# A decode layer's last weight row: two half-row loads, two half-width sums, one store

## The chip, the cores and the metric

The kernel runs on one core of a Trainium2 chip. The metric is the device time of one execution in microseconds (us), lower is better. Times below are medians over runs; a profiled execution is one run with the hardware profiler on. In the profile PE is the matrix engine, PEld its weight loads, DVE the vector engine, ACT the scalar engine, POOL the general-purpose engine and SP the engine that issues most of the transfers.

## The reference

One decode step of a parallel layer: one token `x` of 1024 values, an attention branch with a window of the last 4096 cached positions, and an MLP branch, summed with `x`. Everything is bf16.

```python
x = A_x                                   # [1, 1, 1024]
xn = _layernorm(x)
# attention: 32 heads of 128, 4 key/value heads, window W = 4096 of 65536
q = (xn @ wq)                             # wq [1024, 4096]
p = softmax(q . k[-W:] * 128 ** -0.5)
attn = (p . v[-W:]).reshape(4096) @ wo    # wo [4096, 1024]
# MLP
y = _layernorm(xn)
h = gelu(y @ w1 + b1)                     # w1 [1024, 3584]
mlp = h @ w2 + b2                         # w2 [3584, 1024]
out = x + attn + mlp
```

With one token, every weight is read once and used for one vector: 39.9 MB of weights and cache come in, 2 KB go out.

## The kernel before

The kernel is written engine by engine, with semaphores set and waited for by hand. The order of the code is the order on each engine. Two helpers carry the bookkeeping: `Track.mark` lets an instruction raise its engine's counter, and `C[...]` keeps the count that others wait for. `dw()` makes DVE wait for its own last instruction.

**Loads.** Nearly all loads are issued by SP on one queue, in the order of use: wq, the keys, w1, the values, w2, wo. Each load is split over the 16 DMA engines, and each has a semaphore that counts 16 when all have finished. wo is read as 32 "rows" (`wo_p`, line 150): row j holds, on each of the 128 partitions, 1024 columns, which is 2 KB per partition. It comes in five loads of 16, 9, 4, 2 and 1 rows (`WO_CHUNKS`, line 29). They are issued at lines 394 and 395, after the w1 product has freed the buffers; the first 25 rows go to the buffer `W1`, the last seven to `KT`.

**Products.** wq and w1 are multiplied as they land (`wide_product`, line 286). Scores, softmax and the value product give the attention output `OT`, one column per row of wo. The MLP gives `GT`, one column per row of w2.

**The last sum.** w2's 28 rows and the first 29 rows of wo (`WO_BULK`) go through `bulk` (line 466). Each row is two matmuls of 512 columns with a single weight column; they add up in PSUM bank 6, columns 0 to 511 of the output on partition 0 and 512 to 1023 on partition 32. The last three rows of wo, 29 to 31, take another form (line 490): four matmuls of 256 columns, with the weight column repeated 32 times, so that the four quarters of the output land side by side on the partitions from 0, 32, 64 and 96, in bank 7. That bank was begun by one matmul at line 464 that adds `x` and `b2`: `XB4` holds a quarter of `x` on partitions 0, 32, 64 and 96 and a quarter of `b2` on the partition after each, and `SELX` picks them.

**The end.** When bulk is done, its four quarters are copied from PSUM to the partitions of `BULK`, two by DVE and two by ACT, while the last rows of wo are still landing. When the last matmul of row 31 is done, DVE adds bank 7 and `BULK` into `ORow` in one instruction, and SP stores four partitions of `ORow`, 512 bytes each, to the output:

```python
dve.wait_ge(ACT.sem, C["bulk_a"])
dw()
dve.wait_ge(PE.sem, C["fin"])
C["out"] = d(dve.tensor_tensor(out=ORow[:, :], in0=bank(7, 0, 256), in1=BULK[:, :], op=ALU.add))
sp.wait_ge(DVE.sem, C["out"])
sp.dma_start(out_rows, ORow[0:128:32, :]).then_inc(s_out, 16)
```

Of the kernel before, what the change touches and what calls it, by code (L numbers as in the profile page):

```python
# [5 lines left out]
ALU = mybir.AluOpType  # L6
ACTF = mybir.ActivationFunctionType
AX = mybir.AxisListType

D = 1024  # L10
# [15 lines left out]
WQ_CHUNKS = [8]  # L26
W1_CHUNKS = [8]
W2_CHUNKS = [28]
WO_CHUNKS = [16, 9, 4, 2, 1]
WO_BULK = 29  # L30
WO_W1 = 25


class Track:
# [11 lines left out]
def bass_parallel_sum__sliding_block_cached__mixer_channel_mlp__decode_kernel(  # L46
# [18 lines left out]
    pe, dve, act, pool, sp = nc.tensor, nc.vector, nc.scalar, nc.gpsimd, nc.sync  # L65

    def sems(name, n):
        return [nc.alloc_semaphore(f"{name}{i}") for i in range(n)]

    s_x, s_b1, s_b2, s_out = (nc.alloc_semaphore(n) for n in ("s_x", "s_b1", "s_b2", "s_out"))  # L70
# [1 line left out]
    s_w1 = sems("s_w1", len(W1_CHUNKS))  # L72
    s_k = sems("s_k", NP)
    s_v = sems("s_v", NP)
    s_wo = sems("s_wo", len(WO_CHUNKS))
    s_w2 = sems("s_w2", len(W2_CHUNKS))

    PE = Track(nc, "S_PE")
    DVE = Track(nc, "S_DVE")
    ACT = Track(nc, "S_ACT")  # L80
    POOL = Track(nc, "S_POOL")

    def sb(name, shape, d):
        return nc.alloc_sbuf_tensor(name, shape, d)
# [4 lines left out]
    KT = sb("KT", [128, HKV * W], bf16)  # L89
# [12 lines left out]
    SELX = sb("SELX", [128, 4 * 32], bf16)  # L102
    GMASK = sb("GMASK", [128, HKV], f32)
    XB4 = sb("XB4", [128, 256], bf16)
# [31 lines left out]
    OT = sb("OT", [128, 32], bf16)  # L136
    BULK = sb("BULK", [128, 256], f32)
    ORow = sb("ORow", [128, 256], bf16)
    PS = nc.alloc_psum_tensor("PS", [128, 8 * 512], f32)

    def bank(b, lo=0, n=512):
        return PS[:, b * 512 + lo: b * 512 + lo + n]
# [5 lines left out]
    w1_p = B_w1.rearrange("(p r) n -> p r n", r=KC)  # L148
    w2_p = B_w2.rearrange("(p c) n -> p c n", c=FC)
    wo_p = A_wo.rearrange("(p j) n -> p j n", j=32)  # L150
    out_rows = out.rearrange("b s (a n) -> (b s a) n", a=4)

    C = {}


    def load_rows(dst, src, chunks, width, semaphores, first=0, c0=0, off=0):
        for j, n in enumerate(chunks):
            sp.dma_start(  # L158
                dst[:, off + c0 * width: off + (c0 + n) * width].rearrange("p (c n) -> p c n", c=n),
                src[:, first + c0: first + c0 + n, :],  # L160
            ).then_inc(semaphores[j], 16)
            c0 += n

    load_rows(WA, wq_p, WQ_CHUNKS, NQ, s_wq)
    def d(ins):
        return DVE.mark(ins)

    def dw():
        dve.wait_ge(DVE.sem, DVE.cnt)
# [34 lines left out]
    for G in range(NP):  # L204
# [25 lines left out]
                         op=ALU.add))  # L230
# [55 lines left out]
    def wide_product(weights, chunks, width, semaphores, vec, n, banks, name):  # L286
# [29 lines left out]
        out=TQM[:, :].rearrange("p (g x) -> p g x", g=4), in0=TQ[:, 0:1024:32].unsqueeze(1).to_broadcast([128, 4, 32]),  # L316
        in1=M4[:, :].unsqueeze(2).to_broadcast([128, 4, 32]), op=ALU.mult))
    pe.wait_ge(DVE.sem, C["TQM"])
    pe.wait_ge(POOL.sem, C["selq"])
    last = pe.matmul(bank(6, 16, 128), lhsT=SELQ[:, :], rhs=TQM[:, :], start=True, stop=True)  # L320
# [4 lines left out]
    for a in range(4):  # L325
        dst = QB[32 * a:32 * a + 32, :].rearrange("p (G y) -> p G y", G=2)[:, :, 0:512].rearrange(
            "p G (c z) -> p G c z", c=4)[:, :, :, 32 * a:32 * a + 16]
        src = PS[32 * a:32 * a + 32, 6 * 512 + 16: 6 * 512 + 144].rearrange("p (G x c) -> p G c x", G=2, c=4)
# [6 lines left out]
    for G in range(NP):  # L335
        dve.wait_ge(s_k[G], 16)
        for h in range(2):
            lo = G * PW + h * W
# [3 lines left out]
    for nb in range(4):  # L342
        pe.matmul(bank(nb), lhsT=ML[:, :], rhs=MRow[:, :].unsqueeze(1).to_broadcast([2, 16, 32]),
                  start=True, stop=False)
    pe.wait_ge(DVE.sem, C["QB"])
    pe.wait_ge(ACT.sem, C["QBa"])
    for G in range(NP):
        kg = KT[:, G * PW:(G + 1) * PW].rearrange("p (b c i) -> p c b i", b=PB, c=4)
        for nb in range(4):
            if nb % 2 == 0:  # L350
                pe.wait_ge(DVE.sem, C["kt"][2 * G + nb // 2])
            for c in range(4):
                last = pe.matmul(bank(nb), lhsT=QB[:, G * 512 + c * 128:G * 512 + (c + 1) * 128],  # L353
                                 rhs=kg[:, c, 16 * nb:16 * nb + 16, :], start=False,
                                 stop=(G == NP - 1 and c == 3))
# [29 lines left out]
        out=LR[:, :],  # L385
        in_=PS[0:1, 2 * 512 + 192:2 * 512 + 320].rearrange("o (a m) -> o m a", a=4), axis=AX.X, op=ALU.add))
    dw()
    C["rr"] = d(dve.reciprocal(
        out=RR4[:, :].rearrange("o (q m) -> o q m", q=4), in_=LR[:, :].unsqueeze(1).to_broadcast([1, 4, 32])))
# [3 lines left out]
    sp.wait_ge(PE.sem, C["h"])  # L393
    load_rows(W1, wo_p, WO_CHUNKS[:2], D, s_wo[:2])
    load_rows(KT, wo_p, WO_CHUNKS[2:], D, s_wo[2:], first=WO_W1)

    dve.wait_ge(PE.sem, C["h"])
    dve.wait_ge(s_b1, 16)
    d(dve.tensor_tensor(  # L399
        out=HW32[:, :].rearrange("p (b n) -> p b n", b=2),  # L400
        in0=PS[:, 4 * 512:6 * 512].rearrange("p (b n) -> p b n", b=2)[:, :, 0:QW // 2],
        in1=B1R[:, :].rearrange("p (b n) -> p b n", b=2), op=ALU.add))
# [24 lines left out]
        lhsT=RR4[:, :],  # L427
        rhs=identf[0:1, 0:1], start=True, stop=True))
# [4 lines left out]
    for t in range(32):  # L433
        q = t % 2
        last = pe.matmul(PS[64 * q:64 * q + 64, 3 * 512:4 * 512], lhsT=PT[:, t * 64:(t + 1) * 64], rhs=vb[:, t],  # L435
                         start=(t < 2), stop=(t >= 30))
# [7 lines left out]
        out=OM[:, :].rearrange("p (g d) -> p g d", g=HKV), in0=bank(3).rearrange("p (g d) -> p g d", g=HKV),  # L444
        in1=MG[:, :].unsqueeze(2).to_broadcast([128, HKV, DH]), op=ALU.mult))
# [8 lines left out]
                        in0=bank(2, 352, 128).rearrange("p (q j) -> p q j", q=4),  # L454
                        in1=D4[:, :].unsqueeze(2).to_broadcast([128, 4, 32]), op=ALU.mult))
# [3 lines left out]
                                      axis=AX.X, op=ALU.add))  # L459


    pe.wait_ge(s_x, 16)
    pe.wait_ge(s_b2, 16)
    pe.matmul(bank(7, 0, 256), lhsT=SELX[:, :], rhs=XB4[:, :], start=True, stop=False)

    def bulk(weights, vec, c, lo, first, last):
        for q in range(2):
            ins = pe.matmul(PS[32 * q:32 * q + 1, 6 * 512:7 * 512], lhsT=vec[:, c:c + 1],  # L468
                            rhs=weights[:, lo + q * 512: lo + (q + 1) * 512], start=first, stop=last)
        return ins  # L470

    pe.wait_ge(DVE.sem, C["GT"])
    c = 0
    for j, n in enumerate(W2_CHUNKS):
        pe.wait_ge(s_w2[j], 16)
        for _ in range(n):
            bulk(WA, GT, c, c * D, c == 0, False)
            c += 1
    pe.wait_ge(DVE.sem, C["OT"])
    c = 0  # L480
    for j, n in enumerate(WO_CHUNKS):
        pe.wait_ge(s_wo[j], 16)
        for _ in range(n):
            if c < WO_BULK:
                last = bulk(W1 if c < WO_W1 else KT, OT, c, (c if c < WO_W1 else c - WO_W1) * D, False,
                            c == WO_BULK - 1)
                if c == WO_BULK - 1:
                    C["bulk"] = PE.mark(last)
            else:
                for a in range(4):  # L490
                    lo = (c - WO_W1) * D + a * 256
                    last = pe.matmul(PS[32 * a:32 * a + 32, 7 * 512:7 * 512 + 256],
                                     lhsT=OT[:, c:c + 1].to_broadcast([128, 32]), rhs=KT[:, lo:lo + 256],
                                     start=False, stop=(c == 31))
            c += 1
    C["fin"] = PE.mark(last)

    dve.wait_ge(PE.sem, C["bulk"])
    act.wait_ge(PE.sem, C["bulk"])
    for a in range(4):  # L500
        q = a // 2
        lo = 6 * 512 + (a % 2) * 256
        if q == 0:
            d(dve.tensor_copy(BULK[32 * a:32 * a + 1, :], PS[32 * q:32 * q + 1, lo:lo + 256]))  # L504
        else:
            C["bulk_a"] = ACT.mark(act.activation(out=BULK[32 * a:32 * a + 1, :],  # L506
                                                  in_=PS[32 * q:32 * q + 1, lo:lo + 256], func=ACTF.Copy))
    dve.wait_ge(ACT.sem, C["bulk_a"])
    dw()
    dve.wait_ge(PE.sem, C["fin"])  # L510
    C["out"] = d(dve.tensor_tensor(out=ORow[:, :], in0=bank(7, 0, 256), in1=BULK[:, :], op=ALU.add))  # L511
    sp.wait_ge(DVE.sem, C["out"])
    sp.dma_start(out_rows, ORow[0:128:32, :]).then_inc(s_out, 16)
    sp.wait_ge(s_out, 16)

    return nc
# [28 lines left out]
```

## Time and profile before

| | us |
|---|---|
| median of 3 runs | 101.52 |
| their spread | 101.32 to 101.70 |
| the profiled execution | 101.48 |
| its span, first to last instruction | 99.80 |
| outside the span | 1.68 |

| engine | busy us | share of the span |
|---|---|---|
| PE | 45.1 | 45% |
| PEld | 17.3 | 17% |
| DVE | 38.1 | 38% |
| ACT | 7.3 | 7% |
| POOL | 7.0 | 7% |

A line of the chain of work gives a start, a length and what ran. A line of the timeline gives a start, a length, the engine, the line of the kernel, the operation, output and inputs, shapes and a count; in brackets is the engine's idle time before it and what ended that. A group of instructions gives busy time and mean ns of one after the bar, then idle time. A line of a table of windows gives its stretch and length, then the busy time of PE, PEld, DVE, ACT and POOL, the granted matrix clock, the share of the DMA engines' time that is used, and GB/s. L468 is line 468 of the kernel before.

### The profile page before, as it was taken

How to read it: one execution, taken by the hardware profiler on the slowest of the kernel's cores; microseconds unless marked ns; L12 is line 12 of the kernel's file. 1: busy time of each engine (PE TensorE's matmuls, PEld its weight loads, DVE VectorE, ACT ScalarE, POOL GpSimd, SP SyncE). 2: the span in 40 equal slices, each digit the busy share in tenths (PEclk: the TensorE clock that was granted, in tenths of full speed). 3: DMA queues.
4: the chain of work that ended last, by engine and by line, in shares of the span. 5: the costliest groups of instructions: out<-in, count | busy, mean ns of one | idle time of the engine just before them, and what ended most of it. 6: DMA issues, size and time to landing. Idle time of an engine off the chain costs nothing.

```text
span 99.8 us, 810 instructions
## 1 busy us (share of the span) xinstructions
PE 45.1 (45%) x336; PEld 17.3 (17%) x336; DVE 38.1 (38%) x48; ACT 7.3 (7%) x13; POOL 7.0 (7%) x27
## 2 busy tenths in 40 slices
PE   0000220008934049707271279993400899294760
PEld 0000210003401012202110133450200234041210
DVE  0100443000068999999628176298600000000031
ACT  0000326000022000000000620000000000000020
POOL 6775000000000000000000000000000000000000
PEclk9999999999999655999955555699655579999999
DMA  9399999939999888998699999998889999999910
GB/s 394 158 499 421 475 500 474 420 131 440 433 427 644 368 368 368 598 489 368 259 447 420 433 489 391 598 483 368 368 368 430 420 414 420 440 406 405 393 63 1
DMA packets 1762, 39.89 MB, mean 400 GB/s; under 512 B 208, under 2 KB 224, under 8 KB 480
## 3 DMA queue, kind: packets, MB, share of 16 engines
q1 hardware_dynamic: 1736, 39.85, 93.7%
q8 instruction: 2, 0.03, 0.1%
q10 hardware_dynamic: 24, 0.01, 0.0%
HBM read 39.86 MB, written 0.00 MB: 399 GB/s over the span
## 4 chain that ended last, share of the span: by engine, by line
DMA 53%; DVE 24%; PE 16%; ACT 2%; SPq 1%; issue 1%; DVEq 0%
DMA KT<-in_A_wo_dram 31%; DMA WA<-in_A_wq_dram 22%; DVE KT L339 17%; PE PS L294 11%; PE PS L353 3%; DVE MX L360 2%; ACT WA L375 2%; SPq L158 1%; DVE TQ L312 1%; DVE Q L307 1%; PE PS L371 1%; DVE QB L330 1%; DVE ORow L511 0%; PE PS L362 0%; DVE TQM L315 0%
## 5 line engine op out<-in xcount | busy, mean ns | idle before, releaser
L339 DVE STREAM_TRANSPOSE KT<-KT 128x4096 bf16<-128x4096 bf16 x4 | 17.4, 4413 | 0.0
L353 PE MATMUL PS<-KT,QB 128*128 128x512 bf16 x32 | 9.9, 463 | 9.8 <-DVE KT L339 9.8
L468 PE MATMUL PS<-WA,GT 128*1 128x512 bf16 x56 | 7.8, 448 | 5.8 <-DMA WA<-in_B_w_dram 5.8
L504 DVE COPY BULK<-PS 1x256 f32<-1x256 f32 x2 | 0.8, 413 | 24.0 <-PE PS L468 24.0
L294 PE MATMUL PS<-WA,XNTb 128*32 128x512 bf16 x64 | 5.4, 510 | 8.1 <-DMA WA<-in_A_wq_dram 8.1
L468 PE MATMUL PS<-W,OT 128*1 128x512 bf16 x50 | 5.7, 379 | 3.7 <-DMA W<-in_A_wo_dram 3.7
L294 PE MATMUL PS<-W,YTb 128*32 128x448 bf16 x64 | 6.0, 569 | 0.0
L353 PEld LDWEIGHTS PS<-KT,QB 128*128 128x128 bf16 x32 | 3.2, 109 | 16.1 <-DVE KT L339 12.2
L257 PE MATMUL PS<-XT,onesf 128*128 128x16 f32 x2 | 0.6, 384 | 11.5 <-DVE XT L254 11.5
L307 DVE CAST Q<-PS 128x512 bf16<-128x512 f32 x1 | 0.7, 690 | 12.2 <-PE PS L294 12.2
L468 PEld LDWEIGHTS PS<-WA,GT 128*1 128x1 bf16 x56 | 2.7, 94 | 10.9 <-issue 8.6
L294 PEld LDWEIGHTS PS<-WA,XNTb 128*32 128x32 bf16 x64 | 2.0, 125 | 11.1 <-DMA WA<-in_A_wq_dram 8.3
L375 ACT ACTIVATE WA<-PS,NMB 128x2048 bf16<-128x2048 f32 x1 | 2.0, 1967 | 24.2 <-DVE NMB L373 24.2
L435 PE MATMUL PS<-V,WA 128*64 128x512 bf16 x32 | 3.6, 381 | 0.0
L468 PEld LDWEIGHTS PS<-W,OT 128*1 128x1 bf16 x50 | 2.1, 83 | 7.4 <-issue 2.4
L360 DVE TENSOR_REDUCE MX<-PS 128x1 f32<-128x2048 f32 x1 | 2.3, 2292 | 2.6 <-PE PS L353 2.6
L246 DVE STREAM_TRANSPOSE XT<-XB 128x256 bf16<-128x256 bf16 x1 | 0.6, 625 | 7.0 <-DMA XB<-in_A_x_dram 7.0
L378 DVE STREAM_TRANSPOSE WA<-WA 128x2048 bf16<-128x2048 bf16 x1 | 2.3, 2311 | 2.1 <-ACT WA L375 2.1
L294 PEld LDWEIGHTS PS<-W,YTb 128*32 128x32 bf16 x64 | 2.4, 145 | 3.2 <-issue 3.2
L506 ACT ACTIVATE BULK<-PS 1x256 f32<-1x256 f32 x2 | 0.7, 372 | 28.3 <-PE PS L468 28.2
L257 PEld LDWEIGHTS PS<-XT,onesf 128*128 128x128 f32 x2 | 0.5, 310 | 11.5 <-DVE XT L254 11.5
L399 DVE TENSOR_TENSOR HW<-PS,B1R 128x896 f32<-128x896 f32 x1 | 1.1, 1090 | 2.9 <-PE PS L294 2.9
(95 smaller groups left out, 36.1 us busy)
## 6 DMA issues: line engine op xcount, KB each, us to landing
W<-in_B_w_dram SPq DMA_DIRECT2D x1, 7168.0 KB, 43.6
WA<-in_B_w_dram SPq DMA_DIRECT2D x1, 7168.0 KB, 49.3
KT<-in_A_k_cache_dram SPq DMA_DIRECT2D x2, 2048.0 KB, 23.9
V<-in_A_v_cache_dram SPq DMA_DIRECT2D x2, 2048.0 KB, 50.1
W<-in_A_wo_dram SPq DMA_DIRECT2D x1, 4096.0 KB, 23.0
W<-in_A_wo_dram SPq DMA_DIRECT2D x1, 2304.0 KB, 28.1
KT<-in_A_wo_dram SPq DMA_DIRECT2D x1, 1024.0 KB, 30.2
KT<-in_A_wo_dram SPq DMA_DIRECT2D x1, 512.0 KB, 30.9
```

Source lines behind the costliest of these rows:

```text
L158: sp.dma_start(dst[:, off + c0 * width: off + (c0 + n) * width].rearrange("p (c n) -> p c n", c=n), src[:, first + c0: first + c0 + n, :], ...
L257: C["sum1"] = PE.mark(pe.matmul(bank(6, 0, 16), lhsT=onesf[:, :], rhs=XT16[:, 0:16]))
L294: last = pe.matmul(PS[32 * a:32 * a + 32, banks[b] * 512: banks[b] * 512 + n], lhsT=vec[:, k:k + 1].to_broadcast([128, 32]), rhs=weights[: ...
L307: d(dve.tensor_copy(Q4[:, 0:512], bank(4)))
L339: C["kt"].append(d(dve.transpose(KT[:, lo:lo + W], KT[:, lo:lo + W])))
L353: last = pe.matmul(bank(nb), lhsT=QB[:, G * 512 + c * 128:G * 512 + (c + 1) * 128], rhs=kg[:, c, 16 * nb:16 * nb + 16, :], start=False, st ...
L360: C["mx"] = d(dve.tensor_reduce(out=MX[:, :], in_=PS[:, 0:2048], axis=AX.X, op=ALU.max))
L375: C["exp"] = ACT.mark(act.activation(out=Pb, in_=PS[:, 0:2048], func=ACTF.Exp, bias=NMB[:, 0:1], scale=SCALE, accum_out=RS[:, 0:1]))
L378: C["PT"] = d(dve.transpose(PT, Pb))
L399: d(dve.tensor_tensor(out=HW32[:, :].rearrange("p (b n) -> p b n", b=2), in0=PS[:, 4 * 512:6 * 512].rearrange("p (b n) -> p b n", b=2)[:, ...
L435: last = pe.matmul(PS[64 * q:64 * q + 64, 3 * 512:4 * 512], lhsT=PT[:, t * 64:(t + 1) * 64], rhs=vb[:, t], start=(t < 2), stop=(t >= 30))
L468: ins = pe.matmul(PS[32 * q:32 * q + 1, 6 * 512:7 * 512], lhsT=vec[:, c:c + 1], rhs=weights[:, lo + q * 512: lo + (q + 1) * 512], start=fi ...
```

## The change

The last row of wo, row 31, is loaded in two loads of 512 columns each, with a semaphore each, in place of one of 1024. Rows 29 to 31 are multiplied in the same split: per half of the columns four matmuls of 128 columns (`fin_half`), half 0 into bank 7 and half 1 into bank 5. The partitions from 0, 32, 64 and 96 then hold, for each half, an eighth of the output. DVE adds half 0 as soon as its matmuls are done and half 1 after that, two instructions in place of one, and one store writes both: four partitions with two pieces of 256 bytes each.

So that the bulk sum has its columns in the same places, each `bulk` matmul reads two runs of 256 columns of a row instead of one of 512, and the copies to `BULK` read two runs of 128. `x` and `b2` no longer begin bank 7 before w2's rows; they enter bank 6 in four matmuls of one weight column and 256 columns between w2's last row and wo's first.

```diff
-WO_CHUNKS = [16, 9, 4, 2, 1]
+WO_CHUNKS = [16, 9, 4, 2]
 WO_BULK = 29
 WO_W1 = 25
+DH2 = D // 2
+DQ = D // 8
+HB = (7, 5)
...
-    out_rows = out.rearrange("b s (a n) -> (b s a) n", a=4)
+    out_rows = out.rearrange("b s (h a n) -> (b s a) h n", h=2, a=4)
...
     load_rows(KT, wo_p, WO_CHUNKS[2:], D, s_wo[2:], first=WO_W1)
+    for h in range(2):
+        sp.dma_start(KT[:, 6 * D + h * DH2:6 * D + (h + 1) * DH2], wo_p[:, 31, h * DH2:(h + 1) * DH2]).then_inc(
+            s_wo[4 + h], 16)
...
-    pe.wait_ge(s_x, 16)
-    pe.wait_ge(s_b2, 16)
-    pe.matmul(bank(7, 0, 256), lhsT=SELX[:, :], rhs=XB4[:, :], start=True, stop=False)
-
     def bulk(weights, vec, c, lo, first, last):
+        row = weights[:, lo:lo + D].rearrange("p (h y) -> p h y", h=2)
         for q in range(2):
             ins = pe.matmul(PS[32 * q:32 * q + 1, 6 * 512:7 * 512], lhsT=vec[:, c:c + 1],
-                            rhs=weights[:, lo + q * 512: lo + (q + 1) * 512], start=first, stop=last)
+                            rhs=row[:, :, q * 256:(q + 1) * 256], start=first, stop=last)
+        return ins
+
+    def fin_half(c, h, first, last):
+        for a in range(4):
+            lo = (c - WO_W1) * D + h * DH2 + a * DQ
+            ins = pe.matmul(PS[32 * a:32 * a + 32, HB[h] * 512:HB[h] * 512 + DQ],
+                            lhsT=OT[:, c:c + 1].to_broadcast([128, 32]), rhs=KT[:, lo:lo + DQ], start=first, stop=last)
         return ins
...
+    pe.wait_ge(s_x, 16)
+    pe.wait_ge(s_b2, 16)
+    pe.wait_ge(POOL.sem, C["consts"])
+    for a in range(4):
+        q = a % 2
+        pe.matmul(PS[32 * q:32 * q + 1, 6 * 512 + (a // 2) * 256:6 * 512 + (a // 2) * 256 + 256],
+                  lhsT=SELX[:, 32 * a:32 * a + 1], rhs=XB4[:, :], start=False, stop=False)
     pe.wait_ge(DVE.sem, C["OT"])
...
-                for a in range(4):
-                    lo = (c - WO_W1) * D + a * 256
-                    last = pe.matmul(PS[32 * a:32 * a + 32, 7 * 512:7 * 512 + 256],
-                                     lhsT=OT[:, c:c + 1].to_broadcast([128, 32]), rhs=KT[:, lo:lo + 256],
-                                     start=False, stop=(c == 31))
+                for h in range(2):
+                    fin_half(c, h, c == WO_BULK, False)
             c += 1
-    C["fin"] = PE.mark(last)
+    for h in range(2):
+        pe.wait_ge(s_wo[4 + h], 16)
+        C[f"fin{h}"] = PE.mark(fin_half(31, h, False, True))
...
     for a in range(4):
         q = a // 2
-        lo = 6 * 512 + (a % 2) * 256
+        dst = BULK[32 * a:32 * a + 1, :].rearrange("o (h n) -> o h n", h=2)
+        src = PS[32 * q:32 * q + 1, 6 * 512:7 * 512].rearrange("o (h a n) -> o a h n", h=2, a=2)[:, a % 2]
         if q == 0:
-            d(dve.tensor_copy(BULK[32 * a:32 * a + 1, :], PS[32 * q:32 * q + 1, lo:lo + 256]))
+            d(dve.tensor_copy(dst, src))
         else:
...
     dve.wait_ge(ACT.sem, C["bulk_a"])
     dw()
-    dve.wait_ge(PE.sem, C["fin"])
-    C["out"] = d(dve.tensor_tensor(out=ORow[:, :], in0=bank(7, 0, 256), in1=BULK[:, :], op=ALU.add))
+    for h in range(2):
+        dve.wait_ge(PE.sem, C[f"fin{h}"])
+        C["out"] = d(dve.tensor_tensor(out=ORow[:, h * DQ:(h + 1) * DQ], in0=bank(HB[h], 0, DQ),
+                                       in1=BULK[:, h * DQ:(h + 1) * DQ], op=ALU.add))
     sp.wait_ge(DVE.sem, C["out"])
-    sp.dma_start(out_rows, ORow[0:128:32, :]).then_inc(s_out, 16)
+    sp.dma_start(out_rows, ORow[0:128:32, :].rearrange("p (h n) -> p h n", h=2)).then_inc(s_out, 16)
```

More of the change, by code (lines that the diff above doesn't have):

```diff
@@ L74, in bass_parallel_sum__sliding_block_cached__mixer_channel_mlp__decode_kernel @@
     s_v = sems("s_v", NP)
-    s_wo = sems("s_wo", len(WO_CHUNKS))
+    s_wo = sems("s_wo", len(WO_CHUNKS) + 2)
     s_w2 = sems("s_w2", len(W2_CHUNKS))
@@ L501, in bass_parallel_sum__sliding_block_cached__mixer_channel_mlp__decode_kernel @@
         q = a // 2
-        lo = 6 * 512 + (a % 2) * 256
+        dst = BULK[32 * a:32 * a + 1, :].rearrange("o (h n) -> o h n", h=2)
+        src = PS[32 * q:32 * q + 1, 6 * 512:7 * 512].rearrange("o (h a n) -> o a h n", h=2, a=2)[:, a % 2]
         if q == 0:
-            d(dve.tensor_copy(BULK[32 * a:32 * a + 1, :], PS[32 * q:32 * q + 1, lo:lo + 256]))
+            d(dve.tensor_copy(dst, src))
         else:
-            C["bulk_a"] = ACT.mark(act.activation(out=BULK[32 * a:32 * a + 1, :],
-                                                  in_=PS[32 * q:32 * q + 1, lo:lo + 256], func=ACTF.Copy))
+            C["bulk_a"] = ACT.mark(act.activation(out=dst, in_=src, func=ACTF.Copy))
     dve.wait_ge(ACT.sem, C["bulk_a"])
     dw()
-    dve.wait_ge(PE.sem, C["fin"])
-    C["out"] = d(dve.tensor_tensor(out=ORow[:, :], in0=bank(7, 0, 256), in1=BULK[:, :], op=ALU.add))
+    for h in range(2):
+        dve.wait_ge(PE.sem, C[f"fin{h}"])
+        C["out"] = d(dve.tensor_tensor(out=ORow[:, h * DQ:(h + 1) * DQ], in0=bank(HB[h], 0, DQ),
+                                       in1=BULK[:, h * DQ:(h + 1) * DQ], op=ALU.add))
     sp.wait_ge(DVE.sem, C["out"])
-    sp.dma_start(out_rows, ORow[0:128:32, :]).then_inc(s_out, 16)
+    sp.dma_start(out_rows, ORow[0:128:32, :].rearrange("p (h n) -> p h n", h=2)).then_inc(s_out, 16)
     sp.wait_ge(s_out, 16)
```

## The prediction

> **What bounds the kernel now.** I read the queues, the chain that ended last, then its last five microseconds. From the page, the main load queue (packets, MB, share of 16 engines) and the chain by engine:
>
> ```profile
> q1 hardware_dynamic: 1736, 39.85, 93.7%
> ...
> DMA 53%; DVE 24%; PE 16%; ACT 2%; SPq 1%; issue 1%; DVEq 0%
> ```
>
> The loads fill the 16 DMA engines for 93.7% of the span: the total is set by when the last weights land, plus a tail. The chain in order of time (start, length, what), at its end:
>
> ```profile
> 66.14 31.02 DMA KT<-in_A_wo_dram
> 97.16 0.04 issue
> 97.20 0.32 PE PS L492 x4
> 97.53 0.03 issue
> 97.55 0.05 DVEq L510
> 97.60 0.04 issue
> 97.65 0.42 DVE ORow L511
> ```
>
> The reader is to see that wo's last row lands at 97.16 and that everything after it is serial: four matmuls, 0.12 us of release and wait, an add of 0.42, the store. The timeline of the tail (start, length, engine, what, idle before):
>
> ```profile
> 95.40 1.03 PE L468 MATMUL PS<-KT,OT 128*1 128x512 bf16 x8 [0.43 <-DMA KT<-in_A_wo_dram]
> 96.47 0.77 ACT L506 ACTIVATE BULK<-PS 1x256 f32<-1x256 f32 x2 [28.24 <-PE PS L468]
> 96.47 0.86 DVE L504 COPY BULK<-PS 1x256 f32<-1x256 f32 x2 [24.02 <-PE PS L468]
> 96.61 0.40 PE L492 MATMUL PS<-KT,OT 128*32 128x256 bf16 x8 [0.18 <-DMA KT<-in_A_wo_dram]
> 97.20 0.29 PE L492 MATMUL PS<-KT,OT 128*32 128x256 bf16 x4 [0.19 <-DMA KT<-in_A_wo_dram]
> 97.65 0.42 DVE L511 TENSOR_TENSOR ORow<-PS,BULK 128x256 bf16<-128x256 f32 x1 [0.32 <-PE PS L492]
> 98.10 0.65 SPq L513 DMA_DIRECT2D out_dram<-ORow  x1
> ```
>
> To be seen: DVE is not free while the last row lands. It copies the bulk sum until 96.47 + 0.86 = 97.33, and idles only 0.32 us before the add. Two windows of the same stretch (last columns: clock, DMA share, GB/s):
>
> ```profile
> 94.00:95.00 1.00, 0.97 (x10) 0.20 (x6) 0.00 (x0) 0.00 (x0) 0.00 (x0) 1.00 0.94 363
> 95.00:96.00 1.00, 0.60 (x6) 0.26 (x8) 0.00 (x0) 0.00 (x0) 0.00 (x0) 1.00 0.19 74
> ```
>
> The share falls to 0.19 while rows are still due: in the packet records 14 engines are done by 95.44, and two others alone end at 96.48 and 96.71. The later one sets the last landings.
>
> **The change, part by part.** *Two loads for the last row.* On the engine that ends last a 2048-byte packet takes 84 ns and the next starts 80 ns after it; the store's 512-byte packets take 25 ns, with 22 to the next record. Between these a 1024-byte packet starts every 41 ns or so (bounds 22 and 80). The eight packets of the last row run from 96.07 and their completion record starts at 96.71, 0.45 before the landing at 97.16. With halves: 96.07 + 8 x 0.041 = 96.40, landing 96.85; then 96.41 + 0.33 = 96.74, landing 97.19 (by the bounds 96.88 to 97.80). SP issues one load more, 0.43 us by the row of the loads at L158, at about 66.6. Nothing is behind it on SP until the store at 98.10, and the data come 30 us later: no cost; were that cover gone, 0.47 with the gap.
>
> *Rows 29 and 30 in 16 matmuls of 128 columns.* The second set of four starts 119 ns after the first now, 107 of it columns and 92 to 95 a weight load beneath. With half the columns the pace is 53 to 119 ns a set. From 96.61 the fourth set starts at 96.77 to 96.97, the first half of row 31 at 96.89 to 97.09. A 128-column matmul took 0.23 us at L320, so it ends at 97.12 to 97.32, and is released 0.03 later. The second half starts at 97.23 and is released at 97.49.
>
> *The adds.* One add of 256 columns becomes two of 128. The nearest rows (busy, mean ns):
>
> ```profile
> L511 DVE TENSOR_TENSOR ORow<-PS,BULK 128x256 bf16<-128x256 f32 x1 | 0.4, 424 | 0.3 <-PE PS L492 0.3
> L453 DVE TENSOR_TENSOR OD<-PS,D 128x128 f32<-128x128 f32 x1 | 0.3, 292 | 0.9 <-PE PS L451 0.9
> ```
>
> Halving saves 132 ns, not 212: both halves cost 584. The first also needs the copies. These start when bulk's last matmul is done (96.47, untouched) and end at 97.33; 0.03 release, then 0.05 wait and 0.045 to start as in the chain above: 97.46. It ends at 97.75. The second add is behind it on DVE; its half was ready at 97.49, so it starts 0.034 later (the gap at L443, whose waits were met) at 97.78 and ends at 98.07. Before: 97.65 + 0.42 = 98.07. **So what the earlier first half gives is taken by the copies and by the second add's fixed part: 0.00**, bounds -0.12 (both gaps at their least) and +0.12 (a full wait of 0.12 before the second add, and the first half at its latest). The second half's landing has 0.29 us of slack and is off the path. Behind the first add's wait stand the second add and the store; SP waits for the second add alone.
>
> *Copies and bulk matmuls in two runs.* Bulk's right side becomes two runs of 256 columns. That shape is in the trace, at full pace:
>
> ```profile
> L435 PE MATMUL PS<-V,WA x32: 379/379/403, 64.5 to 67.8; 128*64 128x512 bf16 x32
> ```
>
> 379 ns is what bulk's contiguous ones take: 0. For the copies, L399 reads PSUM in two runs of 448, 896 elements in 1090 ns: (1090 - 424)/640 = 1.04 ns an element beyond L511, and L443's one run gives (692 - 424)/256 = 1.05. No price for a run: 0, at most 0.02.
>
> *x and b2.* One 128x256 matmul (0.42 us at 71.51, not on the chain) goes; four with one weight column come between w2's last row, done at 85.56, and wo's first, which lands at 87.41. Two column groups work side by side, so 2 x 0.11 + 0.17 = 0.4 us, at most 4 x 0.42, inside 1.85 us of waiting: 0. Without that cover, 0.4 us on PE at 87.4, and the wait of 1.81 before the nine-row chunk at 92.86 takes it.
>
> *The store.* Four pieces of 512 bytes become eight of 256 on the same four partitions. The store is issued at 98.10, its first packet starts at 99.35, its last record is at 99.44, and SP is released at 99.79. A second packet per engine: +0.02 at the pace above; its issue, 0.65 us now, may take a little more. I take +0.03; the low bound is 0. The trace holds no 256-byte packet, so the high bound is one more round trip as between record and landing, +0.45.
>
> **Sum:** 0.00 (adds) + 0.01 (copies) + 0.03 (store) = +0.04 us on an execution of 101.48 (99.8 of span, 1.68 around it), which stands 0.04 under the median 101.52 of the runs: 101.52 by the execution, 101.56 by the median. I say 101.55, near the second, since medians are compared.
>
> **Rivals.** *A: the overlap works.* If the copies are done 0.3 us before the first half, the second add starts at about 97.52 and ends at 97.81, -0.26: about 101.3. For it: the halves are released 0.14 to 0.34 apart, room for most of an add. Against it: the copies begin 1.10 us after the four-row chunk lands (95.37) and the last row comes only 1.79 us after that chunk.
>
> *B, slower: the 256-byte pieces.* If a short piece is read, merged and written back at the HBM, each of the two packets on an engine pays a round trip of 0.45 (by the gap from record to landing): +0.45 to +0.90, 101.95 to 102.4, say 102.1. It decides from 0.47 us of added landing on. For it: the store stands alone at the end. Against it: 512-byte pieces are through in 25 ns each, all four within 0.1 us. The Trainium skill ("DMA: Bandwidth & Descriptors", Specifications) says this mechanism begins under 512 bytes; no run here shows it yet.
>
> *C: short load packets cost as much as long ones.* At 80 ns for each of 16, the second half lands at 97.80, is released at 98.10, and the second add ends at 98.43: +0.36, about 101.9. Against it: 512 bytes in 25 ns.
>
> *D: one more instruction fetch.* The trace has two 16384-byte packets on the instruction queue, at 44.65 (1.02 us) and 81.39 (1.11 us); two engines end some 1.1 to 1.4 us behind the rest, which fits one fetch each. 183 and 471 PE instructions had started by then, 288 apart, 682 in all; the change adds 30, so 712, short of 759. If a third fetch did fall on the last engine, the second half would land at 98.26 and end the adds about 0.8 later: 102.4; on another it would be hidden (95.44 + 1.1 is under 96.71). The Trainium skill ("Runtime: NRT & Kernel Launch", Instruction fetch mechanics) gives blocks of 256 instructions; counted so, the next would come at 727, also past the end.
>
> **How the numbers follow.** About 0.5%, 0.51 us, is what a measurement of this kernel can tell from no change. Forecast 0.60 (of it 0.03 faster, 0.05 slower, for the spread of 101.32 to 101.70 and the bounds above), A 0.13 (0.04 faster), B 0.13 (0.11 slower), C 0.06 (0.01 slower), D 0.04 (slower), unnamed 0.04 (halves). Faster 0.09, same 0.68, slower 0.23. The forecast's own range is 101.3 to 101.8. To leave out no more than 2 in 10 it reaches down to A less 0.1 for the spread of runs, and up to B's middle: 101.2 to 102.1.
>
> **What would show it.** Two adds of about 292 ns, the first starting some 0.12 after the copies' end and the second right behind it, not behind PE: the adds as forecast. The first add released by PE would mean that the small matmuls are slower. The second add waiting for PE: C. Idle DVE between two adds: A. From the store's issue to SP's release 1.69 now: over 2.1 is B. A third 16-KB packet, or another gap between the last two engines: D. I am wrong if the last row lands over 0.29 us later than now, or the four-row chunk, which starts the copies, moves at all.

## The result, and the profile after

The changed kernel takes 100.92 us, the kernel before 101.48 in the same series: a ratio of 0.9941, 95% interval 0.9932 to 0.9949, so 0.6% faster. The ratio leaves out two of the changed kernel's 22 runs, 102.20 and 102.79 us, which were in a slow state. The result is under the range on record (101.2 to 102.1) and in the case that had the least chance, faster at 0.09.

Every timed run also has a span, from the first to the last instruction. Splitting each time into span and the rest gives the first reading, and it is not the one the prediction was built on. For the changed kernel the mean span is 99.59 us, and the median outside is 1.26. For the kernel before they are 99.73 to 99.81 and 1.67, over the series of the experiments. **Only 0.14 to 0.22 us of the gain is inside the span; 0.41 lies outside it**, where the profile lists no work.

In the two profiled executions the outside is 1.68 and 1.40. The trace's record of the granted clock ends 1.99 us after the last instruction before, and 1.71 after the change. Both differences are 0.28: the time went from behind the last instruction, not from ahead of the first. The two go together in every run below too: in all 18 profiled executions that record ends 0.30 to 0.31 us later than the outside.

The page of the changed kernel: span, busy time by engine with its count of instructions, the load queue, the chain by engine.

```profile
span 99.6 us, 842 instructions
...
PE 45.7 (46%) x351; PEld 17.6 (18%) x351; DVE 38.2 (38%) x49; ACT 7.3 (7%) x13; POOL 7.1 (7%) x27
...
q1 hardware_dynamic: 1884, 39.85, 94.0%
...
DMA 53%; DVE 25%; PE 16%; ACT 2%; issue 1%; SPq 1%; DVEq 0%
```

The loads are as full as before. DVE has 49 operations where it had 48; this turns out to matter more than anything else here. The end of its chain in order of time:

```profile
95.23 0.04 issue
95.27 1.05 PE PS L471 x8
96.32 0.02 issue
96.34 0.41 DVE BULK L521
96.76 0.03 issue
96.79 0.42 DVE BULK L521
97.21 0.00 issue
97.21 0.05 DVEq L527
97.26 0.04 issue
97.31 0.49 DVE ORow L528 x2
```

Before, the chain went from the last row's landing to its matmuls and one add. Now it goes from the four-row chunk (95.23) through the bulk sum and DVE's two copies to the adds: the copies hold the first add, as forecast. But the two adds together take 0.49 us, not 0.62. The timeline of the same stretch:

```profile
96.34 0.86 DVE L521 COPY BULK<-PS 1x256 f32<-1x256 f32 x2 [25.11 <-PE PS L471]
96.53 0.23 PEld L478 LDWEIGHTS PS<-KT,OT 128*32 128x32 bf16 x16 [0.74 <-DMA KT<-in_A_wo_dram]
96.53 0.90 PE L478 MATMUL PS<-KT,OT 128*32 128x128 bf16 x24 [0.23 <-DMA KT<-in_A_wo_dram]
96.92 0.10 PEld L478 LDWEIGHTS PS<-KT,OT 128*32 128x32 bf16 x4 [0.15 <-DMA KT<-in_A_wo_dram]
97.19 0.10 PEld L478 LDWEIGHTS PS<-KT,OT 128*32 128x32 bf16 x4 [0.18 <-DMA KT<-in_A_wo_dram]
97.31 0.49 DVE L528 TENSOR_TENSOR ORow<-PS,BULK 128x128 bf16<-128x128 f32 x2
97.82 0.68 SPq L531 DMA_DIRECT2D out_dram<-ORow  x1
```

The halves start PE at 96.92 and 97.19, and the store is issued at 97.82 instead of 98.10. Two windows (last columns: clock, DMA share, GB/s) show the same thinning load as before:

```profile
94.00:95.00 1.00, 0.89 (x10) 0.17 (x4) 0.00 (x0) 0.00 (x0) 0.00 (x0) 1.00 0.99 373
95.00:96.00 1.00, 0.73 (x8) 0.26 (x8) 0.00 (x0) 0.00 (x0) 0.00 (x0) 1.00 0.27 98
```

And the adds beside the row that priced them, L453 of the kernel before and L459 of this one (busy, mean ns of one):

```profile
L528 DVE TENSOR_TENSOR ORow<-PS,BULK 128x128 bf16<-128x128 f32 x2 | 0.5, 286 | 0.1
...
L459 DVE TENSOR_TENSOR OD<-PS,D 128x128 f32<-128x128 f32 x1 | 0.3, 293 | 0.6 <-PE PS L457 0.6
```

Each add costs what was forecast (291 and 280 ns), yet busy time is 0.49, less than their sum: the second starts at 97.515, 0.083 before the first one's end at 97.598.

### The profile page after: what moved, and what is told of

It is laid out like the page before. It is cut to its first block, busy times and chain, and to the rows that moved or that the text cites. A ratio compares the mean times of both kernels' runs of the same rounds, so it can differ in the third digit from the quotient of the medians.

```text
span 99.6 us, 842 instructions
## 1 busy us (share of the span) xinstructions
PE 45.7 (46%) x351; PEld 17.6 (18%) x351; DVE 38.2 (38%) x49; ACT 7.3 (7%) x13; POOL 7.1 (7%) x27
## 4 chain that ended last, share of the span: by engine, by line
DMA 53%; DVE 25%; PE 16%; ACT 2%; issue 1%; SPq 1%; DVEq 0%
DMA KT<-in_A_wo_dram 31%; DMA WA<-in_A_wq_dram 22%; DVE KT L342 18%; PE PS L297 11%; DVE MX L363 2%; ACT WA L378 2%; PE PS L356 2%; DVE TQ L315 1%; PE PS L471 1%; DVE BULK L521 1%; DVE Q L310 1%; DVE QB L333 1%; PE PS L374 1%; SPq L161 1%; DVE ORow L528 0%
## 5 line engine op out<-in xcount | busy, mean ns | idle before, releaser
L356 PE MATMUL PS<-KT,QB 128*128 128x512 bf16 x32 | 9.4, 445 | 8.8 <-DVE KT L342 8.8
L471 PE MATMUL PS<-WA,GT 128*1 128x512 bf16 x56 | 8.6, 481 | 7.2 <-DMA WA<-in_B_w_dram 7.2
L521 DVE COPY BULK<-PS 1x256 f32<-1x256 f32 x2 | 0.8, 414 | 25.1 <-PE PS L471 25.1
L297 PE MATMUL PS<-WA,XNTb 128*32 128x512 bf16 x64 | 6.1, 565 | 8.1 <-DMA WA<-in_A_wq_dram 8.1
L297 PE MATMUL PS<-W,YTb 128*32 128x448 bf16 x64 | 5.0, 494 | 0.0
```

The lines of the kernel that those rows point to most:

```text
L297: last = pe.matmul(PS[32 * a:32 * a + 32, banks[b] * 512: banks[b] * 512 + n], lhsT=vec[:, k:k + 1].to_broadcast([128, 32]), rhs=weights[: ...
L521: d(dve.tensor_copy(dst, src))
```

## The experiments

Times are medians of series in which the kernel before ran on the same chip. "Span" is the mean of the runs, "outside" the median of time less span.

**One: x and b2 alone.** The kernel before, with its early matmul replaced by four into the bulk sum.

```diff
-    pe.matmul(bank(7, 0, 256), lhsT=SELX[:, :], rhs=XB4[:, :], start=True, stop=False)
...
+    for a in range(4):
+        q = a // 2
+        pe.matmul(PS[32 * q:32 * q + 1, 6 * 512 + (a % 2) * 256:6 * 512 + (a % 2) * 256 + 256],
+                  lhsT=SELX[:, 32 * a:32 * a + 1], rhs=XB4[:, :], start=False, stop=False)
```

> The kernel before with one part of the change alone: x and b2 enter the bulk sum between w2 and wo, the early matmul is gone, everything else stays. Theory T (the gain is made in the tail, where the second add starts before the first is finished): no difference from before, 101.5 us, within 0.1. Rival M (the move of x and b2 and what it does ahead of the tail or after the last instruction is where the 0.40 us come from that the tail does not show): about 101.1, with the four-row chunk landing about 0.12 earlier or the time outside the span 0.3 shorter.

Measured: 101.44 against 101.37 (ratio 1.0007, 0.9997 to 1.0018), span 99.80, outside 1.65. The move is worth nothing, as forecast, and rival M falls.

**Two: one load for the last row.**

```diff
-    for h in range(2):
-        sp.dma_start(KT[:, 6 * D + h * DH2:6 * D + (h + 1) * DH2], wo_p[:, 31, h * DH2:(h + 1) * DH2]).then_inc(
-            s_wo[4 + h], 16)
+    sp.dma_start(KT[:, 6 * D:7 * D], wo_p[:, 31, :]).then_inc(s_wo[4], 16)
```

> The changed kernel with wo's last row in one load again; the halves, the two adds and the store stay. Theory T with the half load as its cause: the first half is released some 0.3 us later and the first add with it, so the adds end 0.15 to 0.25 later, 101.1 to 101.2 us. Rival L (the halves' landing does not matter, since the copies hold the first add): the first add at the copies' end as in the changed kernel, 100.9 us, at most 0.05 more.

Measured: 101.04 (0.9968, 0.9956 to 0.998), span 99.83, outside 1.23. The line of the adds in its timeline (start, length; in brackets DVE's idle time and what ended it):

```profile
97.51 0.49 DVE L526 TENSOR_TENSOR ORow<-PS,BULK 128x128 bf16<-128x128 f32 x2 [0.34 <-PE PS L476]
```

The first add now waits 0.34 us for PE, and the span gives back all that the changed kernel had won: the half load is needed, and rival L falls. The pair still takes 0.49, although both halves were ready, so the 208 ns from start to start is the adds' own pace and not a wait for PE.

**Three: one add for both halves.** The banks of the halves are swapped so that one instruction can read them in order.

```diff
-    for h in range(2):
-        dve.wait_ge(PE.sem, C[f"fin{h}"])
-        C["out"] = d(dve.tensor_tensor(out=ORow[:, h * DQ:(h + 1) * DQ], in0=bank(HB[h], 0, DQ),
-                                       in1=BULK[:, h * DQ:(h + 1) * DQ], op=ALU.add))
+    dve.wait_ge(PE.sem, C["fin1"])
+    C["out"] = d(dve.tensor_tensor(
+        out=ORow[:, :].rearrange("p (h n) -> p h n", h=2),
+        in0=PS[:, 4 * 512:8 * 512].rearrange("p (h n) -> p h n", h=2)[:, :, 512:512 + DQ],
+        in1=BULK[:, :].rearrange("p (h n) -> p h n", h=2), op=ALU.add))
```

> The changed kernel with one add of two runs of 128 columns after both halves are done; two loads and the store stay. Theory T: the add starts after the second half's release (97.49 on the changed kernel's clock) plus 0.1 of wait and start and takes 0.42 to 0.43, so it ends about 0.2 later than the two adds: 101.1 us. Rival M: the two adds are worth nothing, 100.9.

Measured: 101.46 (1.0015, 1.0003 to 1.0027). The span is 99.79, so 0.2 longer than the changed kernel's, as theory T had it. But the whole is 0.54 longer: the outside went back to 1.67. Neither theory had that. This kernel keeps the loads, matmuls, semaphores and store of the changed one and has one DVE instruction less.

**Four: the second add waits for the first.**

```diff
     for h in range(2):
+        if h:
+            dw()
         dve.wait_ge(PE.sem, C[f"fin{h}"])
```

> The changed kernel with one wait more: the second add waits until the first has finished. Theory T (the second add starts 0.21 us after the first one's start, 0.08 before its end): the overlap goes, the second add starts 0.03 to 0.1 after the first one's end, +0.1 to +0.2, 101.05 us. Rival (the second add was released by its own matmuls and the overlap is only how the profile draws it): no change, 100.9.

Measured: 101.10 (0.9972, 0.9959 to 0.9984), span 99.72, outside 1.40.

```profile
97.35 0.62 DVE L530 TENSOR_TENSOR ORow<-PS,BULK 128x128 bf16<-128x128 f32 x2
```

0.62 instead of 0.49: the overlap is real and worth 0.13 us, and the span grows by just that (99.72 after 99.59). The outside moved again, to a third value, with one wait more on DVE. From here the question was the outside.

**Five to eight: DVE's number of instructions.** Unread one-column copies are put at DVE's start, where it waits for x, or one on ACT; nothing else changes.

```diff
     dve.wait_ge(POOL.sem, C["ident"])
+    dve.tensor_copy(DUM[:, 0:1], identf[:, 0:1])
```

> The kernel before with one more instruction on DVE: a copy of one column at the start, where DVE waits for x; nothing reads it. Theory N (the time outside the span, 1.66 us for the kernel before and 1.26 for the changed one, goes by the number of DVE's instructions, of which the changed kernel has one more): outside 1.25, span as before, about 101.0 us. Rival E (it goes by how DVE's work ends, two adds of which the second overlaps the first): outside 1.66, 101.4.

> The kernel before with two such copies on DVE. Theory N: as in the changed kernel with one wait more, outside about 1.40, 101.15 us. Rival E: 1.66, 101.4.

> The changed kernel with one such copy at DVE's start, so two DVE instructions more than before. Theory N: outside about 1.40 with the span of the changed kernel, 101.05 us. Rival E: 1.26 outside, 100.9.

> The kernel before with one instruction more on ACT, a copy of one column at about 13 us where ACT waits. Theory N for DVE alone: no change, outside 1.66, 101.4 us. Rival (any engine's count does it): outside moves by 0.1 or more. Rival E: 1.66.

Measured: **the kernel before with one useless copy takes 101.00 against 101.40** (0.9964, 0.9952 to 0.9976), span 99.74, outside 1.28. Two copies: 101.19, outside 1.39. The changed kernel with one copy: 100.94, span 99.55, outside 1.41. One more on ACT: 101.47, outside 1.69. Theory N holds in all four: the outside goes by DVE's count, whichever kernel it is and wherever the extra instruction stands, and rival E falls. PE's count does not set it: the third kernel has the changed one's 712 PE instructions and 1.67 outside, the fifth has the old 682 and 1.28.

**Nine to eleven: further counts, and one add at the count of the changed kernel.** The ninth is the changed kernel with two copies, the tenth the kernel before with four, the eleventh the third kernel with one copy.

> The changed kernel with two unread one-column copies on DVE at its start: 59 DVE instructions. Theory N (the time outside the span goes by the place at which DVE's instructions end: 1.66 at 56, 1.26 at 57, 1.40 at 58): the span of the changed kernel, 99.6, and an outside of its own between 1.2 and 1.7, 100.8 to 101.25 us. Rival (only one step at 57 and then a slow rise with the count): about 1.5, 101.1.

> The kernel before with four such copies on DVE: 60 DVE instructions. If the outside time goes by the place within groups of four instructions: 1.66 as at 56, 101.4 us. If it rises from 57 on: above 1.4, about 101.3. If it stays low: 1.26, 101.0.

> The changed kernel with one add in place of two, as in the third experiment, and one unread copy on DVE, so that it has as many DVE instructions as the changed kernel, 57. Theory N and T together: outside 1.26, and a span 0.2 longer than the changed kernel's, 99.8: 101.05 us. If the outside time went by the two adds: 1.66, 101.45.

Measured: 101.13 (span 99.52, outside 1.57), 101.34 (99.80, 1.55), 101.10 (99.76, 1.29). The eleventh settles the third: with the count restored, one add costs 0.17 of span (0.2 expected), and the outside is back at 1.29. The ninth fits theory N, whose range left little out, and its rival (1.5) as well; the tenth fits the rise (above 1.4) and not the groups of four (1.66). In the records of the ninth and tenth stands something new after the last instruction: an instruction packet of 8192 bytes, at 100.90 and at 101.32. Both traces end when that packet ends, at 101.32 in the ninth and 101.78 in the tenth.

**Twelve: five copies on the kernel before.**

> The kernel before with five unread one-column copies on DVE: 61 DVE instructions. Outside the span so far: 1.67 us at 56, 1.26 at 57, 1.40 at 58, 1.57 at 59, 1.55 at 60. If it goes by groups of four instructions: about 1.3 as at 57, 101.1 us. If it drifts up with the count after the step at 57: 1.55 to 1.7, 101.4 us.

Measured: 101.96 (1.0046, 1.003 to 1.0062): outside 1.28, as groups of four had it and not the rise, but a span of 100.68, which neither had. SP's waits in that kernel, then in the kernel before (total us, times, longest):

```profile
SPq L520 <- DMA out_dram<-ORow: 2.0, 1, 2.0
```

```profile
SPq L514 <- DMA out_dram<-ORow: 1.0, 1, 1.0
```

The store takes 1 us longer. The DMA queues of the twelfth kernel from 97 us to its end show what shares the engines with it (packets, MB, share):

```profile
q14 instruction: 1, 0.01, 0.7%
q1 hardware_dynamic: 8, 0.00, 0.2%
```

One instruction packet of 8192 bytes runs from 99.24 to 99.63, among the eight packets of the store. Three of the store's data packets start by 99.24, the fourth at 99.62; SP is released at 100.61. In the kernel before, the four start within 0.06 us. So 0.35 of the 0.96 us is the late fourth packet. The other 0.6 lies between its completion record and SP's release (0.96 us, 0.35 before); the thirteenth kernel below shows the same (0.89), and no row gives the reason.

**Thirteen to sixteen: 62, 64, 76 and 77 DVE instructions.** The kernel before with six, eight and twenty copies, the changed kernel with twenty.

> The kernel before with six unread one-column copies on DVE: 62 DVE instructions. With five, an instruction packet of 8192 bytes ran at 99.24, among the store's packets, and the span grew by 0.9. Theory F (DVE's own instruction fetch, due when DVE reaches a fixed place of its program, is what moves the end): the packet comes one instruction earlier, so at about 97 to 99, and if it still shares an engine with the store the span stays near 100.6; outside as at 58, 1.40: 101.0 to 102.0 us. Rival (the packet with five was something else): no such packet, 101.2 us.

> The kernel before with eight copies: 64 DVE instructions. Theory F: the packet comes when DVE gets three instructions ahead of its last add, at the copies of the bulk sum (96 to 98), before the store; the span is back near 99.8 or a little over; outside 1.55 to 1.67 if groups of four hold: 101.4 us. Rival: no packet.

> The kernel before with twenty copies: 76 DVE instructions. Theory F: the packet comes at about 70 us, where DVE is 15 instructions from its end, and costs at most its 0.4 us on one of 16 engines; nothing in the tail. Groups of four: outside 1.67 as at 56, 101.4 us. If the outside time is what a fetch near the end leaves over, it is the least seen or below: 1.2, 100.9 us.

> The changed kernel with twenty copies: 77 DVE instructions. Theory F: packet at about 70 us; groups of four: outside 1.26 as at 57, 100.9 us, no gain over the changed kernel. If the outside time is left over from a fetch near the end: below 1.2, 100.6 to 100.8 us.

Measured: 101.91 (1.005, span 100.67, outside 1.26), 101.46 (1.0003, 100.21, 1.27), 100.93 (0.9947, 0.9929 to 0.9965; 99.68, 1.24) and 100.84 (0.994, 0.9924 to 0.9957; 99.60, 1.27). Theory F holds in its main point: the packet of 8192 bytes stands at 99.13, 98.83, 67.01 and 65.10. It follows DVE's count, to earlier times, though the times on record were off by up to 5 us, and the outside that groups of four gave for 62 and 64 (1.40, 1.55 to 1.67) did not come. With 62 it still hits the store. With 64 it comes ahead of the store's packets, and DVE pauses before its last add, in the chain of the fourteenth kernel:

```profile
97.25 0.04 issue
97.29 0.32 PE PS L501 x4
97.61 0.03 issue
97.64 0.05 DVEq L519
97.69 0.48 issue
98.17 0.42 DVE ORow L520
```

Between the wait and the add, where the kernel before spends 0.045 us, DVE stands for 0.48 with nothing to wait for. It does not wait for the packet's data: the packet starts at 98.83, 0.24 after the add has ended. That DVE asks for its instructions in this pause would fit, but the profile does not show it. With 76 the packet is one among the loads. The queues of the fifteenth kernel from 66 to 68 us:

```profile
q1 hardware_dynamic: 15, 0.86, 101.4%
q14 instruction: 1, 0.01, 1.0%
```

and it costs nothing that can be seen. All counts together:

| DVE instructions | kernels | span | outside | the 8192-byte packet after the first instruction |
|---|---|---|---|---|
| 56 | before; 1, 3, 8 | 99.7 to 99.8 | 1.65 to 1.69 | none in the record |
| 57 | changed; 2, 5, 11 | 99.6; 99.7 to 99.8 | 1.23 to 1.29 | none in the record |
| 58 | 4, 6, 7 | 99.5 to 99.8 | 1.39 to 1.41 | none in the record |
| 59 | 9 | 99.5 | 1.57 | after the last instruction, 100.90 |
| 60 | 10 | 99.8 | 1.55 | after the last instruction, 101.32 |
| 61 | 12 | 100.7 | 1.28 | in the store, 99.24 |
| 62 | 13 | 100.7 | 1.26 | in the store, 99.13 |
| 64 | 14 | 100.2 | 1.27 | after the last add, 98.83 |
| 76 and 77 | 15, 16 | 99.7; 99.6 | 1.24; 1.27 | 67.01; 65.10 |

The counts include seven waits that are instructions of their own (eight in the fourth kernel) and a drain at the start. Six or seven packets of 8192 bytes stand ahead of the first instruction in every trace. Groups of four fall: 58 and 62, 60 and 64 differ. What holds is that from 61 on, when the packet lies ahead of the end, the outside is 1.24 to 1.28, and that up to 60 it is anything from 1.23 to 1.69. No packet shows at 56 or 57.

The traces record what the listings above leave out: updates of semaphores, also behind the last instruction. The pattern there is the same in all 18 profiled executions: five updates of semaphore 2 and one of each of some 230 to 250 others, in five groups of neighbouring numbers; then five more updates of semaphore 2, and four last ones. **In the four kernels with 56 DVE instructions the four last ones come 0.51 us after the five; in all others 0.10 to 0.11. That is where the 0.41 lies.**

With 58 a shorter pause stands one step earlier: the fourth of the second five comes 0.16 to 0.21 us after the third, where 56, 57 and all from 61 on have 0.04 to 0.06 (59 has 0.07, 60 has 0.18). With 59 and 60 one of the five groups starts 0.73 and 0.87 us after the last instruction, 0.30 to 0.32 in all others. So a closing sequence runs behind the kernel, and as DVE's count falls from 60 to 56, all but 57 show a pause that stands later in it. Where a pause and the packet are both on record (59, 60, 64), the packet starts 0.48 to 0.66 us after the pause ends. By that, an estimate, the packet of the kernels with 56 and 58 would start behind the end of their traces. That DVE has to fetch the closing instructions fits all of this; the profile does not list them, so it is argued and not shown. Why 57 shows no pause at all is open.

The sixteenth kernel, 100.84, is not to be told from the changed kernel, 100.92: its count had been a good one already.

## Why the prediction was wrong

**Right.** The halves land at 96.87 and 97.15 (forecast 96.85 and 97.19); a 1024-byte packet starts every 42 ns (41). The small matmuls come in sets 56 to 65 ns apart (53 to 119). Bulk's two-run matmuls take 379 ns, the two-run copies 413 and 414: no price. The move of x and b2 costs nothing (one). The copies hold the first add, which starts 0.106 after their end (0.13). From the store's issue to SP's release it is 1.73 us, 1.69 before: +0.04 (0.03), and rival B, which would have given 0.45 or more, is excluded. The Trainium skill ("DMA: Bandwidth & Descriptors", Specifications) puts a read-modify-write under 512 bytes; a 256-byte packet of this store takes 15 to 18 ns where a 512-byte one took 25 to 27, and no such cost shows here. Rival C is excluded by the landings of the halves. Two landings were read late from the profile before, wo's first as 87.41 (its semaphore is full at 87.30) and the four-row chunk as 95.37 (95.35); no term of the sum hangs on them.

**Wrong, in the span.** The step is "it starts 0.034 later", the gap taken from L443. There the second instruction waits for the first one's result. Two adds that do not depend on each other start 0.208 apart, 0.083 before the first one's end; the wait of the fourth kernel brings it to 0.325. The mis-sized term is that start: 0.034 after was -0.083 after, 0.12 in all. The adds end 0.59 after the copies' end, where one add took 0.745: -0.15, and with the store -0.11. The spans give 0.14 to 0.22. In the profiled pair the four-row chunk also landed 0.12 earlier (95.23, 95.35 before), which the prediction had named as a sign of being wrong. That is no part of the change: among the profiled kernels that keep the old loads it landed anywhere from 94.84 to 95.47.

**Wrong, around the span.** The step is "101.48 (99.8 of span, 1.68 around it)", where the 1.68 was taken as fixed. It went to 1.26, -0.41, the greater part of the result, because the second add makes 57 DVE instructions of 56. Twenty useless copies on the kernel before give 0.52 us, nearly as much as the whole change. No view of the profile before lists what runs in this time. What was there to see was the 1.68 itself and the second add as an added instruction, and the sum gave that no price from either side.

**The rivals.** A came nearest for the span (-0.14 to -0.22 of its -0.26), by a road it did not name: not copies done earlier, but adds that overlap. D had the right kind of event, an instruction fetch that collides with the tail, and looked for it on PE, with its 682 instructions; the runs point to DVE, with 56, and to a gain and not a loss. Its count of PE instructions was off as well: a third packet of 16384 bytes did come in three of the eight profiled executions with 712 PE instructions, once all 712 had started and short of 759. It came at 97.46 in the seventh kernel and 97.39 in the ninth, whose spans, 99.55 and 99.52, show no cost. In the third it came at 101.13, behind the last instruction, and the trace ends with it; that execution had 2.22 us outside the span, where the median of its runs is 1.67. The Trainium skill ("Runtime: NRT & Kernel Launch", Instruction fetch mechanics) says that crossing a block of instructions is mostly hidden. At 76 the trace agrees (nothing to see); at 61 the store that meets the packet takes 0.96 us longer, and at 64 DVE pauses for 0.48 us ahead of it.

## What to carry to other kernels

Split a measured time into span and outside before explaining it; a kernel of 100 us can win or lose 0.4 us behind its last instruction and 0.9 in its store by one instruction more or less on DVE. When an edit changes an engine's instruction count, run the old kernel with as many useless instructions on that engine, in a place where it waits: if this moves the time, the edit's gain is not all the edit's. And two instructions of DVE that do not depend on each other can be closer than the sum of their durations, so a gap has to be taken from a pair with the same dependence.

## What the runs showed of the hardware

An instruction packet of 8192 bytes that follows DVE's count takes 0.32 to 0.46 us on a DMA engine. Its time follows DVE's place in the program: 67 us with 76 instructions, 98.8 with 64, behind the last instruction with 59 and 60. Where it ran among the store's packets, issue to release of the store took 2.65 us (61) and 2.51 (62) and not 1.69. Where an instruction packet came behind the last instruction (3, 9, 10), the trace ended with it, 0.23 to 0.54 us after the last semaphore update; all others ended 0.11 to 0.12 us after that update. The same two adds take 0.49 us, or 0.62 with a wait for the first between them. The copies at L521 do not overlap in this way (0.03 between the first one's end and the second's start), although nothing in the code makes the second wait. One difference is that the copies write to partitions 0 and 32 and both adds to the partitions from 0; no run tests whether it matters.
